# Logits of the second layer moved from TensorE to VectorE sums, with paired evictions, conditional weight splits and later ranks, in a pooled attention with two routed layers

## The chip, the cores and the metric

One core of one Trainium2 chip runs the whole program. The metric is the device time of one execution in microseconds; the median of three runs is given, and one profiled execution is read beside it. TensorE is PE in the profile, its weight load PEld, VectorE DVE, ScalarE ACT, GpSimd POOL and SyncE SP.

## The reference

An attention over keys and values that are pooled by eight gives x of 4608 tokens by 512. Two layers of eight experts follow, each expert 512 to 1024 to 512. Layer 1 gives a token to the expert of the largest logit; layer 2 passes a token by where its skip score is not positive, and adds to it otherwise.

```python
logits = x @ w_gate + modality_bias[modality_id]      # layer 1
e_idx = np.argmax(logits, axis=1)
...
h = np.maximum(x[mask] @ w1[e], 0.0)
out[mask] = gate_w[mask, None] * (h @ w2[e])
...
skip_score = x @ w_skip                               # layer 2, x = layer 1's output
do_compute = skip_score > 0
logits = xc @ w_gate
e_idx = np.argmax(logits, axis=1)
...
out[do_compute] = xc + y
```

Layer 2 so needs nine columns for every output row of layer 1: eight gate logits and the skip score.

## The kernel before, in words

The attention runs first; the routing of layer 1 begins beside it. A layer's tokens are sorted on chip into blocks of 256 rows (two halves, t = 0 and 1) that belong to one expert each, with the most used expert first. Layer 1 has 19 blocks with this input, from three experts. `Layer.second` does block 1, `Layer.body` the blocks from 2 on, `Layer.rec` those whose number is only known at run time; `first2` does layer 2's block 0 behind the last block of layer 1.

All products are made in fp32 as three products of high and low parts: each of w1, w2, x and h is split into a rounded high part (w1h, w2h, xh, hh, a copy on ACT) and the rest (w1l, w2l, xl, hl, a subtraction on DVE, for some w1l on POOL). `gemm1` (L1352) makes for each of eight slices f of the hidden width 12 matmuls of 128x256 into one of two PSUM buffers, from which ACT takes hh and DVE hl. `gemm2` (L1405) makes 24 matmuls of 128x512 for each half. In between, `xT` (L1311) transposes the next block's rows, and `split_w1`, `split_w2` (L1299, L1305) split the weights, in every block, even where the expert and so the raw weights stay the same: the loads of raw weights are conditional on a change of expert (chg), the splits are not. A half block skips its second `gemm2`.

The order of all instructions is written by hand: the program records them as the Python code runs, `body` calls `gemm1(i, f)`, then the split of w2, then a piece of the work that was deferred from the block before, for each f. The deferred work of layer 1's block i-1 (`deferred1`, L1561) is layer 2's gating for its outputs: `tr` transposes a half with PE (L1572), ACT and DVE split it (x2h, x2l); `mm` multiplies it with the gating weights W9s, high and low parts side by side in 64 columns (L1585); `mm2` transposes the result back (L1593) and DVE adds its two parts; `pick1` and `pick2` find on POOL and DVE the expert of each row (rt_mx and rt_my are the two maxima of DVE, M the one-hot choice, rt_i the running counts of POOL); x2 goes to DRAM and rows that skip are scattered to the output. `rank`, at the end of the block, multiplies M and rt_i with triangular and all-one matrices on PE (L874, L875, result R), DVE turns R into positions (L883 to L891), and POOL makes from them the one-hot tiles OB (L903).

```python
return {0: lambda: tr(0), 1: lambda: tr(1), 3: mm, 4: mm2, 5: pick1, 8: pick2, 9: rank}
```

The numbers are the f of gemm1 behind which each piece stands; 8 is the start and 9 the end of the second product. `body` gathers the rows of block i+1 at the start of block i (L1294), into one of two buffers xg. Layer 2 uses the same body with halves of a block chosen at run time, and no deferred work.

## Time and profile before

| | us |
|---|---|
| median of three runs | 990.66 (989.79 to 994.31) |
| the profiled execution's own time | 995.08 |
| its span in the trace | 993.3 |
| PE busy | 938.0 (94%) |
| DVE busy | 650.9 (66%) |
| ACT busy | 537.6 (54%) |
| POOL busy | 580.6 (58%) |

The profiled execution is one run of the program on the chip. Its mean granted clock of TensorE is 0.978 of full speed. The attention takes the first quarter, layer 1 runs to some 705 us, layer 2 to the end. A row of a timeline gives the start, the duration, the engine, the line, the operation, output and inputs with their tiles, the shape, how many alike follow in one row, and in brackets the idle time before it and what ended it. Matmuls are pipelined: their durations overlap, and the distance between two starts is what one costs.

### The profile page before, as it was taken

How to read it: one execution, taken by the hardware profiler on the slowest of the kernel's cores; microseconds unless marked ns; L12 is line 12 of the kernel's file. 1: busy time of each engine (PE TensorE's matmuls, PEld its weight loads, DVE VectorE, ACT ScalarE, POOL GpSimd, SP SyncE). 2: the span in 40 equal slices, each digit the busy share in tenths (PEclk: the TensorE clock that was granted, in tenths of full speed). 3: DMA queues.
4: the chain of work that ended last, by engine and by line, in shares of the span. 5: the costliest groups of instructions: out<-in, count | busy, mean ns of one | idle time of the engine just before them, and what ended most of it. 6: DMA issues, size and time to landing. Idle time of an engine off the chain costs nothing.

```text
span 993.3 us, 19808 instructions
## 1 busy us (share of the span) xinstructions
PE 938.0 (94%) x6535; PEld 841.5 (85%) x6535; DVE 650.9 (66%) x1533; ACT 537.6 (54%) x1137; POOL 580.6 (58%) x809
## 2 busy tenths in 40 slices
PE   5899999899999999999999999999898999999995
PEld 4699889788898888888899899988886897988984
DVE  4486786777666666666666676667546667667555
ACT  2465556544465555555566656546422555566553
POOL 4754697303587777677777777766634444342442
PEclk7799999999999999999999999999999999999998
DMA  9998865510111111442223521214422664481251
GB/s 225 216 253 228 230 181 161 182 55 23 44 60 66 57 63 58 137 144 72 71 74 101 186 75 61 70 60 155 153 76 79 222 219 163 132 282 34 96 173 40
DMA packets 86900, 123.66 MB, mean 124 GB/s; under 512 B 14143, under 2 KB 51007, under 8 KB 86760
## 3 DMA queue, kind: packets, MB, share of 16 engines
q1 hardware_dynamic: 75224, 94.31, 31.2%
q0 software_dynamic: 10320, 27.59, 8.9%
q8 instruction: 65, 1.06, 0.5%
q14 instruction: 75, 0.61, 0.2%
q10 hardware_dynamic: 1216, 0.08, 0.1%
HBM read 181.29 MB, written 39.48 MB: 222 GB/s over the span
## 4 chain that ended last, share of the span: by engine, by line
PE 69%; DMA 11%; DVE 7%; POOL 6%; issue 5%; ACT 2%; DVEq 0%; POOLq 0%; ACTq 0%
PE ps_g L1360 27%; PE ps_g L1412 23%; DMA out_dram<-o,o2i 5%; PE ps_av L368 4%; DMA xg<-xd,gidx 4%; PE ps_s L301 3%; PE ps_x L1314 2%; PE ps_lg L1585 2%; POOL OB L903 2%; PE ps_et L348 2%; PE ps_x L1572 1%; DMA xg<-x2s,gidx 1%; PE ps_s L327 1%; POOL w1l L1302 1%; PE ps_q L280 1%
## 5 line engine op out<-in xcount | busy, mean ns | idle before, releaser
L1360 PE MATMUL ps_g<-xh,w1h 128*128 128x256 f32 x896 | 262.0, 292 | 6.7 <-DVE hl L1364 3.8
L1360 PE MATMUL ps_g<-xl,w1h 128*128 128x256 f32 x896 | 253.4, 283 | 0.7 <-DVE xl L1318 0.7
L1360 PE MATMUL ps_g<-xh,w1l 128*128 128x256 f32 x896 | 253.6, 283 | 0.0
L1302 POOL TENSOR_TENSOR w1l<-w1r,w1h 128x512 fp32r<-128x512 f32 x105 | 134.3, 1303 | 103.8 <-ACT w1h L1301 103.0
L1412 PE MATMUL ps_g<-w2h,hh 128*128 128x512 f32 x464 | 189.7, 409 | 0.9 <-DVE rs_v L1038 0.5
L1363 ACT ACTIVATE hh<-ps_g 128x256 fp32r<-128x256 f32 x224 | 86.1, 384 | 188.9 <-PE ps_g L1360 183.3
L1412 PE MATMUL ps_g<-w2h,hl 128*128 128x512 f32 x464 | 183.4, 395 | 0.0
L1412 PE MATMUL ps_g<-w2l,hh 128*128 128x512 f32 x464 | 182.9, 394 | 0.0
L1360 PEld LDWEIGHTS ps_g<-xh,w1h 128*128 128x128 f32 x896 | 170.4, 190 | 14.5 <-issue 4.8
L1308 DVE TENSOR_TENSOR w2l<-w2r,w2h 128x512 fp32r<-128x512 f32 x232 | 160.4, 696 | 20.5 <-ACT w2h L1307 3.8
L1360 PEld LDWEIGHTS ps_g<-xl,w1h 128*128 128x128 f32 x896 | 170.8, 191 | 1.3 <-DVE xl L1318 1.1
L1360 PEld LDWEIGHTS ps_g<-xh,w1l 128*128 128x128 f32 x896 | 170.4, 190 | 0.0
L1364 DVE SCALAR_TENSOR_TENSOR hl<-ps_g,hh 128x256 fp32r<-128x256 f32 x224 | 94.9, 424 | 81.9 <-ACT hh L1363 79.9
L1307 ACT CAST w2h<-w2r 128x512 fp32r<-128x512 f32 x232 | 140.8, 613 | 2.6 <-DVE gidxf L1041 2.5
L1301 ACT CAST w1h<-w1r 128x512 fp32r<-128x512 f32 x240 | 136.8, 618 | 5.7 <-DMA w1r<-in_moe_w_dram 5.7
L903 POOL TENSOR_SCALAR OB<-iota,BB,pay 128x128 bf16<-128x128 bf16 x126 | 111.3, 891 | 20.9 <-DVE BB L891 18.5
L1302 DVE TENSOR_TENSOR w1l<-w1r,w1h 128x512 fp32r<-128x512 f32 x135 | 106.8, 814 | 9.3 <-ACT w1h L1301 9.1
L1412 PEld LDWEIGHTS ps_g<-w2h,hl 128*128 128x128 f32 x464 | 87.4, 188 | 21.6 <-DVE hl L1382 1.3
L1412 PEld LDWEIGHTS ps_g<-w2h,hh 128*128 128x128 f32 x464 | 87.6, 189 | 18.9 <-ACT hh L1381 1.5
L1412 PEld LDWEIGHTS ps_g<-w2l,hh 128*128 128x128 f32 x464 | 87.8, 189 | 16.1
L1318 DVE TENSOR_TENSOR xl<-ps_x,xh 128x512 fp32r<-128x512 f32 x64 | 43.9, 687 | 50.4 <-ACT xh L1317 50.3
L1557 POOL DMA_INDIRECT out_dram<-o,o2i x21 | 23.6, 1122 | 71.8 <-DVE o2i L1556 33.7
(280 smaller groups left out, 1487.0 us busy)
## 6 DMA issues: line engine op xcount, KB each, us to landing
w1r<-in_moe_w_dram SPq DMA_DIRECT2D x128, 512.0 KB
w2r<-in_moe_w_dram SPq DMA_DIRECT2D x128, 512.0 KB
x2s<-x SPq DMA_DIRECT2D x19, 522.0 KB
v<-in_v_dram SPq DMA_DIRECT2D x48, 192.0 KB
xd<-x SPq DMA_DIRECT2D x16, 520.0 KB
q_sb<-in_q_dram SPq DMA_DIRECT2D x16, 512.0 KB
kt<-in_k_dram SPq DMA_DIRECT2D x32, 144.0 KB
x2s<-OBx SPq DMA_DIRECT2D x16, 261.0 KB
```

What stands on the lines that cost most here:

```text
L301: nc.tensor.matmul(ps[p0:p1, hp // 2, (hp % 2) * 144:(hp % 2) * 144 + 144], lhsT=t[:, hp, p0:p1], rhs=KB[b % NR][:, hp, :], start=(hp % 2 ...
L368: nc.tensor.matmul(ps[p0:p1, j // 3, o:o + 2 * VW], lhsT=t[:, j, p0:p1], rhs=VB[b % NR][:, j].rearrange("p i w -> p (i w)"), start=(j % 3 ...
L903: e.tensor_scalar(g.ob(c)[:, i, :], g.iota, r.BB[:, c:c + 1], r.pay[:, i, c:c + 1], ALU.is_equal, ALU.mult)
L1301: self.nc.scalar.copy(self.w1h[f], raw)
L1302: (eng or self.nc.vector).tensor_tensor(self.w1l[f], raw, self.w1h[f].bitcast(F32), ALU.subtract)
L1307: self.nc.scalar.copy(self.w2h[f], raw)
L1308: (eng or self.nc.vector).tensor_tensor(self.w2l[f], raw, self.w2h[f].bitcast(F32), ALU.subtract)
L1318: nc.vector.tensor_tensor(self.xl[i % 2][:, :, 128 * t:128 * t + 128], ps, hi.bitcast(F32), ALU.subtract)
L1360: nc.tensor.matmul(ps, lhsT=a[f][:, k, :], rhs=b[:, k, :], start=(n == 0), stop=(n == 11))
L1363: nc.scalar.activation(out=self.hh[f], in_=ps, func=ACTF.Relu)
L1364: nc.vector.scalar_tensor_tensor(self.hl[f], in0=ps, scalar=0.0, in1=self.hh[f].bitcast(F32), op0=ALU.max, op1=ALU.subtract)
L1412: nc.tensor.matmul(ps, lhsT=a[f][:, tt], rhs=b[f], start=(n == 0), stop=(n == 23))
```

## The change

- Layer 2's nine columns are computed by DVE: for each half and column one `tensor_tensor_reduce` (`logit`) multiplies 128x512 rows of x2 with a broadcast row of the gating weights and sums them, 18 for a block. They stand in a list `todo` with their picks, from which `drip` takes some behind each f of gemm1 and gemm2. `settle` empties it for a block before its buffer x2 is written again. The gating weights are loaded during the attention, transposed once, and broadcast from DRAM to all partitions (`W9`, 9 by 512).
- hh and hl leave PSUM for two f at a time (128x512), and there are three PSUM buffers in place of two.
- In layer 1 the rows are gathered two blocks ahead; xh and xl have one buffer in place of two.
- In layer 1 w1 and w2 are split only if the next block has another expert (`split`), inside a branch on ACT and DVE; all w1l of layer 1 are now on DVE.
- `rank` of block i-1's outputs moves from the end of block i into block i+1, to gemm1's f = 4.
- In `first2` the second half's logits of the last block are made on PE (`late_logits`), the splits of w2 come three f later, two ranks stand in gemm1 (f = 4) and gemm2 (f = 2), and the transposes of block 1 inside gemm2(0, 0).
- In layer 2 the last split of w1 of a half block goes to POOL; the output tile o has two fixed buffers.

```diff
+        V.tensor_tensor(r.split, r.chg, r.end, ALU.add)
...
+        self.xh[1], self.xl[1] = self.xh[0], self.xl[0]
+        self.gate[1] = p.tile([128, 2], F32, name="gate1")
         for i in range(2):
             self.x2[i] = p.tile([128, 2, W2C], F32, name=f"x2{i}")
-        self.W9 = p.tile([128, 4, E + 1], F32, name="W9")
-        self.W9s = p.tile([128, 4, 64], F32R, name="W9s")
+            self.lg2[i] = p.tile([128, 2, E + 1], F32, name=f"lg2{i}")
+            self.dsi[i] = p.tile([128, 2], I32, name=f"dsi{i}")
+            self.rti[i] = p.tile([128, 2, E], BF16, name=f"rti{i}")
...
+        self.W9 = p.tile([128, E + 1, DM], F32, name="W9")
+        junk = self.sp.tile([128, DM], F32, tag="hr", name="junk", bufs=1)
+        self.junk = junk.bitcast(BF16)[:, 0:DM]
+        self.o2 = [p.tile([128, DM], F32, name=f"o2{t}") for t in range(2)]
...
+        nc, g = self.nc, self.g
+        ps = self.ps_t("ps_w")
+        for k in range(4):
+            nc.tensor.transpose(ps[0:E + 1, k, :], g.w9c[:, k, :], g.ident)
+        w = self.o2[0]
+        nc.scalar.copy(w[0:E + 1, :], ps[0:E + 1].rearrange("p k n -> p (k n)"))
+        nc.sync.dma_start(out=g.w9, in_=w[0:E + 1, :])
+        nc.sync.dma_start(out=self.W9, in_=g.w9.unsqueeze(0).to_broadcast([128, E + 1, DM]))
...
+    def load_split(self, i):
+        ET = mybir.EngineType
+        self.anew = self.nc.values_load(self.g.r1.split[0:1, i:i + 1], min_val=0, max_val=1,
+                                        engines=[ET.Activation, ET.DVE])
+    def split_w1_if(self, fs):
+        with self.tc.If(self.anew > 0):
+            for f in fs:
+                self.split_w1(f)
+    def split_w2_if(self, fs):
+        with self.tc.If(self.anew > 0):
+            for f in fs:
+                self.split_w2(f)
...
+            if f % 2 == 0:
+                self.ps_pair = self.ps_1("ps_g1")
+            out, whole = self.ps_pair[:, T * (f % 2):T * (f % 2) + T], self.ps_pair
+            hh, hl = (t[f // 4][:, f % 4 - 1:f % 4 + 1, :].rearrange("p f n -> p (f n)")
+                      if f % 2 else None for t in (self.hh4, self.hl4))
+        else:
+            out, whole, hh, hl = ps, ps, self.hh[f], self.hl[f]
...
+        if hh is not None:
+            nc.scalar.activation(out=hh, in_=whole, func=ACTF.Relu)
+            nc.vector.scalar_tensor_tensor(hl, in0=whole, scalar=0.0, in1=hh.bitcast(F32),
+                                           op0=ALU.max, op1=ALU.subtract)
-        return self.pp.tile([128, 512], F32, tag="g1", name=name, bufs=2)
+        return self.pp.tile([128, 512], F32, tag="g1", name=name, bufs=3)
...
+            self.settle(i - 2)
...
+            self.todo += self.posts(i, t)
...
+    def late_logits(self, i):
+        nc = self.nc
+        ps = self.ps_t("ps_x2")
+        for k in range(4):
+            nc.tensor.transpose(ps[:, k, :], self.x2[i % 2][:, 1, 128 * k:128 * k + 128],
+                                self.g.ident)
+        xt = self.o2[1].rearrange("p (k n) -> p k n", k=4)
+        nc.scalar.copy(xt, ps)
+        yield
+        lg = self.pp.tile([128, E + 1], F32, tag="m", name="ps_lg")
+        for k in range(4):
+            nc.tensor.matmul(lg, lhsT=xt[:, k, :], rhs=self.g.w9c[:, k, :], start=(k == 0),
+                             stop=(k == 3))
+        nc.vector.tensor_copy(self.lg2[i % 2][:, 1, :], lg)
...
+        self.gather(g.r2.gidx0, 2, 1, g.x2s[0:16 * T, :])
+        late = self.late_logits(n - 1)
         for f in range(8):
             self.gemm1(n, f)
+            for x in todo[2 * f:2 * f + 2 if f < 7 else None]:
+                x[2]()
+            if f in (1, 3):
+                next(late)
+            if f == 4:
+                self.rank_all(ranks)
+            if f == 5:
+                first()
+            if f > 2:
+                self.split_w2(f - 3)
+        second()
+        for f in range(5, 8):
             self.split_w2(f)
-            if f in d:
-                d.pop(f)()
-        self.gather(g.r2.gidx0, 2, 1, g.x2s[0:16 * T, :])
         self.gates1(1, self.sp)
-        d.pop(8)()
-        self.gemm2(0, 0, self.epilogue2)
-        for t in range(2):
-            self.xT(1, t, self.ps_t("ps_x"))
+        self.gemm2(0, 0, self.epilogue2, {2: self.rank_all,
+                                          3: lambda: self.xT(1, 0, self.ps_t("ps_x")),
+                                          5: lambda: self.xT(1, 1, self.ps_t("ps_x"))})
         self.gates2(1, self.sp)
         self.gemm2(0, 1, self.epilogue2)
-        d.pop(9)()
+        self.scatter(n - 1, 1)
...
+            P.tensor_copy(x2[:, :, DM:DM + E + 1], lg)
...
+            V.tensor_reduce(out=mx, in_=lg[:, :, 0:E], axis=AX.X, op=ALU.max)
+            P.tensor_tensor(eq, lg[:, :, 0:E], bc(mx), ALU.subtract)
+            P.tensor_scalar(eq, eq, 0.0, None, ALU.is_ge)
+            P.tensor_tensor(eq, eq, g.desc.unsqueeze(1).to_broadcast([128, 2, E]), ALU.mult)
...
+            V.tensor_reduce(out=my, in_=eq, axis=AX.X, op=ALU.max)
+            P.tensor_tensor(eq, eq, bc(my), ALU.subtract)
+            P.tensor_scalar(M, eq, 0.0, None, ALU.is_ge)
...
+            self.ranks.append(i)
...
+    def rank(self, i):
+        nc, g, r2 = self.nc, self.g, self.g.r2
+        V = nc.vector
+        M, I = r2.M[:, 2 * i:2 * i + 2, :], self.rti[i % 2]
+        B = r2.BB[:, 2 * i:2 * i + 2]
+        R = self.pp.tile([128, 2, E], F32, tag="m", name="R")
...
+        nc.gpsimd.tensor_tensor(r2.RH[:, 2 * i:2 * i + 2], ra, B, ALU.subtract)
+        for _ in route_places(self.tc, g, r2, 2 * i, 2, nc.gpsimd):
+            pass
...
+    def logit(self, i, t, e):
+        self.nc.vector.tensor_tensor_reduce(
+            out=self.junk, in0=self.x2[i % 2][:, t, 0:DM], in1=self.W9[:, e, :], scale=1.0,
+            scalar=0.0, op0=ALU.mult, op1=ALU.add, accum_out=self.lg2[i % 2][:, t, e:e + 1])
+    def posts(self, i, t):
+        l = [(i, True, partial(self.logit, i, t, e)) for e in range(E + 1)]
+        if t == 0 and i > 0:
+            l.insert(5, (i - 1, False, partial(self.scatter, i - 1, 1)))
+        if t == 1:
+            first, second = self.picks(i)
+            l += [(i, True, first), (i, True, second)]
+        return l
+    def settle(self, i):
+        while any(x[0] <= i for x in self.todo):
+            self.drip()
+    def drip(self, n=1):
+        while n > 0 and self.todo:
+            _, cost, f = self.todo.pop(0)
+            f()
+            n -= cost
...
+        ahead = 2 if self.n == 1 else 1
+        if i + ahead < NBLK:
+            self.gather(i + ahead)
...
+    def body1(self, i, end):
+        m = self.m
+        late = i == self.n_static - 1
+        ranks = m.ranks
+        m.ranks = []
+        for f in range(8):
+            m.gemm1(i, f)
+            if f in (1, 3):
+                m.split_w2_if(range(2 * f - 2, 2 * f + 2))
+            m.drip(((0, 0, 1, 1, 1, 1, 2, 2) if late else (1, 1, 1, 2, 1, 2, 1, 1))[f])
+            m.g.bg.tick()
+            if f == 4:
+                m.rank_all(ranks)
+        if late:
             m.gather2(i + 1)
             m.load_w1_parts(2, m.e2, end, range(4))
-        self.finish(i, d, end, full, turn)
+        full = self.load_full(i)
+        more = i + 1 < NBLK or end is not None
+        if i + 1 < NBLK:
+            self.load_w2(i + 1)
+        if end is not None:
+            m.load_w2_parts(2, m.e2, end)
+        def next_x(t):
+            if t == 0 and end is not None:
+                m.gates1(i + 1, m.sp)
+            m.xT(i + 1, t, m.ps_t("ps_x"))
+            if t == 1:
+                m.gates2(i + 1, m.sp)
+        if more:
+            m.load_split(i + 1)
+            if end is None:
+                m.gates1(i + 1, m.sp)
+            m.split_w1_if(range(8))
+        at = {f: m.drip for f in (0, 1, 3, 5, 6)}
+        if more and not late:
+            at.update({2: lambda: next_x(0), 4: lambda: next_x(1)})
+        m.gemm2(i, 0, self.epilogue, at)
+        if more and late:
+            m.drip(4)
+            next_x(0)
+            next_x(1)
+            m.drip(3)
+        else:
+            m.drip(7)
+        with m.tc.If(full > 0):
+            m.gemm2(i, 1, self.epilogue)
```

PE in a block of layer 1. Before, the rank (R, from M and rt_i) opens the first product, whose matmuls (ps_g) are broken by two groups of four transposes and by the logits:

```order
L874 MATMUL R<-M_666,trim 128x16
L875 MATMUL R<-rt_i,ones 128x16
L1360 MATMUL ps_g_3639<-xh_2114,w1h_2120 128x256
...
L1572 MATMUL ps_x_3656<-ident,x_2998 128x128 x4
L1360 MATMUL ps_g_3665<-xh_2114,w1h_2120 128x256
...
L1572 MATMUL ps_x_3682<-ident,x_2998 128x128 x4
...
L1585 MATMUL ps_lg<-x2h,W9s 64x256
...
L1585 MATMUL ps_lg<-x2l,W9s 64x256
L1360 MATMUL ps_g_3734<-xh_2114,w1h_2532 128x256
...
L1593 MATMUL ps_lt<-ident,lt 128x64 x2
L1360 MATMUL ps_g_3756<-xh_2114,w1h_2532 128x256
```

Now nothing but the rank of an earlier block stands between the matmuls, behind f = 4:

```order
L1400 MATMUL ps_g_4008<-xh_2117,w1l_2538 128x256
L1696 MATMUL R<-M_669,trim 128x16
L1697 MATMUL R<-rti_3003,ones 128x16
L1400 MATMUL ps_g_4008<-xh_2117,w1h_2537 128x256
```

The transposes and logits are gone, and R moved from the block's start into its first product.

DVE in the same block, around the first product's start. Before, each hl (128x256) is followed by a w2l:

```order
L1364 SCALAR_TENSOR_TENSOR hl_2535<-ps_g_4844,hh_2534 128x256
L1308 TENSOR_TENSOR w2l_2991<-w2r_2539,w2h_2990 128x512
L1364 SCALAR_TENSOR_TENSOR hl_2535<-ps_g_4861,hh_2534 128x256
L1308 TENSOR_TENSOR w2l_2993<-w2r_2539,w2h_2992 128x512
L1336 TENSOR_REDUCE g_mx<-xg_2113 128x2
L1337 TENSOR_TENSOR gd_3004<-xg_2113,g_mx 128x2x8
L842 TENSOR_REDUCE rt_my<-rt_eq 128x2
L1318 TENSOR_TENSOR xl_2115<-ps_x,xh_2114 128x4x128
L1302 TENSOR_TENSOR w1l_2121<-w1r_2118,w1h_2120 128x512
```

Now hl is 128x512, the splits stand behind a branch, and the logits (ISA, each with the read of its 128x1 sum) fill the queue:

```order
L1717 ISA lg_3001 128x1
L1405 SCALAR_TENSOR_TENSOR hl_2126<-ps_g_6008,hh_2125 128x512
L1335 COMPARE_AND_BRANCH
...
L1335 UNCONDITIONAL_BRANCH x2
L1717 ISA junk,lg_3001<-x_3000,W_3008 128x512
L1717 ISA lg_3001 128x1
...
L1325 TENSOR_LOAD split_650
L1370 TENSOR_REDUCE g_mx<-xg_2116 128x2
L1330 COMPARE_AND_BRANCH
L1320 TENSOR_TENSOR w1l_2124<-w1r_2120,w1h_2123 128x512 x2
...
L1330 UNCONDITIONAL_BRANCH x2
L1717 ISA junk,lg_3001<-x_3000,W_3008 128x512
...
L1352 TENSOR_TENSOR xl_2118<-ps_x,xh_2117 128x4x128
```

The subtractions of w1l and w2l moved into the branch; in front of xl there are logits in place of hl and w2l.

PE in `first2`, in the second product of layer 2's block 0. Before, the next block's transposes stand between the halves and the rank behind both:

```order
L1412 MATMUL ps_g_14767<-w2h_2992,hl_2535 128x512
L1314 MATMUL ps_x<-ident,xg_2721 128x128 x8
L1412 MATMUL ps_g_14816<-w2h_2540,hh_2122 128x512
...
L1412 MATMUL ps_g_14816<-w2h_2992,hl_2535 128x512
L874 MATMUL R<-M_666,trim 128x16
L875 MATMUL R<-rt_i,ones 128x16
```

Now the rank comes behind the third slice of the first half, ahead of the transposes:

```order
L1453 MATMUL ps_g_14603<-w2h_2720,hl_2126 128x512
L1696 MATMUL R<-M_669,trim 128x16
L1697 MATMUL R<-rti_3007,ones 128x16
L1453 MATMUL ps_g_14603<-w2h_2722,hh_2125 128x512
...
L1453 MATMUL ps_g_14603<-w2h_2722,hl_2126 128x512
L1348 MATMUL ps_x<-ident,xg_2726 128x128 x4
L1453 MATMUL ps_g_14603<-w2h_2724,hh_2539 128x512
```

The rank moved ahead by some 40 matmuls, and the transposes into the first half.

## Rows read from the trace of the kernel before

**Rows 1.** Busy time per engine in two stretches of one block.

```profile
core 0: us, PE busy (x) PEld busy (x) DVE busy (x) ACT busy (x) POOL busy (x), PEclk, DMA share, GB/s
438.40:464.30 25.90, 25.90 (x174) 23.33 (x173) 16.70 (x38) 15.28 (x32) 18.98 (x30) 1.00 0.24 83
541.80:567.60 25.80, 25.80 (x173) 23.27 (x172) 16.58 (x38) 15.29 (x32) 18.92 (x30) 1.00 0.59 192
```

**Rows 2.** Timeline of PE in one block of layer 1.

```profile
start us, us, engine line op out<-in xcount [idle before <-releaser]
446.23 0.60 PE L1572 MATMUL ps_x<-ident,x 128*128 128x128 f32 x4
...
446.90 0.28 PE L1360 MATMUL ps_g<-xh,w1l 128*128 128x256 f32 x1
...
451.37 0.28 PE L1585 MATMUL ps_lg<-x2h,W9s 128*64 128x256 f32 x1
...
452.31 0.28 PE L1360 MATMUL ps_g<-xh,w1h 128*128 128x256 f32 x1
...
453.63 0.28 PE L1360 MATMUL ps_g<-xh,w1l 128*128 128x256 f32 x1
...
454.44 0.28 PE L1360 MATMUL ps_g<-xh,w1l 128*128 128x256 f32 x1
```

**Rows 3.** Timeline of DVE in the same block; columns as in Rows 2.

```profile
445.12 0.17 DVE L885 TENSOR_REDUCE rt_ra<-rt_rk 128x2 f32<-128x16 f32 x1
445.33 0.17 DVE L887 CAST rt_ri<-rt_ra 128x2 int32<-128x2 f32 x1
...
447.41 0.69 DVE L1308 TENSOR_TENSOR w2l<-w2r,w2h 128x512 fp32r<-128x512 f32 x1
448.02 0.69 DVE L1578 TENSOR_TENSOR x2l<-ps_x,x2h 128x512 fp32r<-128x512 f32 x1
...
463.09 1.52 DVE L1302 TENSOR_TENSOR w1l<-w1r,w1h 128x512 fp32r<-128x512 f32 x1
```

**Rows 4.** Timeline of DVE in layer 2; columns as in Rows 2.

```profile
772.12 0.74 DVE L1553 SCALAR_TENSOR_TENSOR o<-ps_g,gate,xg 128x512 f32<-128x512 f32 x1
772.78 0.14 DVE L1556 TENSOR_TENSOR o2i<-xg,emptyf 128x1 int32<-128x1 f32 x1
772.85 0.16 DVE L1349 TENSOR_REDUCE g_su<-gd 128x2 f32<-128x18 f32 x1
```

**Rows 5.** Timeline of POOL, layer 1 and first2; columns as in Rows 2.

```profile
446.75 3.82 POOL L903 TENSOR_SCALAR OB<-iota,BB,pay 128x128 bf16<-128x128 bf16 x4
...
456.01 0.26 POOL L1606 TENSOR_SCALAR d_pos<-x 128x2 f32<-128x2 f32 x1 [2.60 <-DVE x L1597]
...
457.85 0.22 POOL L832 TENSOR_TENSOR rt_eq<-x,rt_mx 128x16 f32<-128x16 f32 x1
...
458.51 0.52 POOL L836 TENSOR_TENSOR rt_eq<-rt_eq,desc 128x16 f32<-128x16 f32 x1
...
731.26 0.21 POOL L844 TENSOR_TENSOR rt_eq<-rt_eq,rt_my 128x16 f32<-128x16 f32 x1 [3.07 <-DVE rt_my L842]
...
733.00 0.19 POOL L870 CAST rt_i<-carry 128x8 bf16<-128x8 f32 x1
```

**Rows 6.** DVE groups by shape: xcount | busy us, mean ns | idle.

```profile
L1159 DVE SCALAR_TENSOR_TENSOR tokf<-rs_v,rs_lo 128x52 f32<-128x52 f32 x2 | 0.4, 213 | 0.1
...
L999 DVE SCALAR_TENSOR_TENSOR er_a<-RH,er_a 128x18 f32<-128x18 f32 x1 | 0.2, 178 | 0.0
```

**Rows 7.** Waits of PE by what they were for: us, times, longest.

```profile
PE ps_g L1360 <- DVE hl L1364: 3.8, 5, 1.1
```

**Rows 8.** PE timeline, block 13 to 14; columns as in Rows 2.

```profile
568.77 0.17 PE L874 MATMUL R<-M,trim 128*128 128x16 bf16 x1 [0.28 <-POOL M L848]
570.55 0.17 PE L875 MATMUL R<-rt_i,ones 128*128 128x16 bf16 x1 [1.61 <-POOL rt_i L870]
```

**Rows 9.** Stretch of PE after that; columns as in Rows 1.

```profile
572.00:575.00 3.00, 3.00 (x16) 3.00 (x16) 2.93 (x4) 1.44 (x3) 2.80 (x4) 0.50 0.23 87
```

**Rows 10.** PE timeline, step into first2; columns as in Rows 2.

```profile
708.22 0.55 PE L1360 MATMUL ps_g<-xh,w1h 128*128 128x256 f32 x1 [2.58 <-issue]
```

More of the change, by code (lines that the diff above doesn't have):

```diff
@@ L1117, in route_blocks @@
     yield
+    if r.split is not None:
+        V.tensor_tensor(r.split, r.chg, r.end, ALU.add)
+        yield
 def route_slots(tc, g, r, sp, pp, pace=1):
@@ L1521, in gather_next @@
         self.gather(gi, 0, i, g.x2s[0:16 * T, :])
+    def late_logits(self, i):
[6 more added lines that the diff above has]
+        nc.scalar.copy(xt, ps)
+        yield
+        lg = self.pp.tile([128, E + 1], F32, tag="m", name="ps_lg")
[3 more added lines that the diff above has]
+        nc.vector.tensor_copy(self.lg2[i % 2][:, 1, :], lg)
+        yield
     def first2(self, n):
         nc, g = self.nc, self.g
+        ranks = self.ranks
+        self.ranks = []
+        todo = [x for x in self.todo[:-11]]
+        first, second = self.picks(n - 1)
+        self.todo = []
         nc.vector.tensor_copy(self.gate0, self.gate[n % 2])
@@ L1619, in pick2, with second @@
+        def second():
+            eq, val = st["eq"], st["val"]
+            my = tile("rt_my")
+            V.tensor_reduce(out=my, in_=eq, axis=AX.X, op=ALU.max)
+            P.tensor_tensor(eq, eq, bc(my), ALU.subtract)
+            P.tensor_scalar(M, eq, 0.0, None, ALU.is_ge)
+            P.tensor_tensor(M, M, bc(val), ALU.mult)
+            for c in range(2):
+                P.tensor_tensor(r2.carry, r2.carry, M[:, c, :], ALU.add)
+                P.tensor_copy(I[:, c, :], r2.carry)
             nc.sync.dma_start(
@@ new lines, in rank_all @@
+    def rank_all(self, ranks=None):
+        ranks = self.ranks if ranks is None else ranks
+        while ranks:
+            self.rank(ranks.pop(0))
+    def logit(self, i, t, e):
[10 more added lines that the diff above has]
+        return l
@@ L1684, in second @@
         self.gather(2)
+        if self.n == 1:
+            self.gather(3)
         if self.n == 2:
@@ L1723, in body @@
             m.load_w1_parts(2, m.e2, end, range(4))
-        d = self.deferred(i - 1, nc.gpsimd) if self.deferred is not None else {}
-        def gemm1():
-            for f in range(8):
-                m.gemm1(i, f)
-                m.split_w2(f)
-                if f in d:
-                    d.pop(f)()
-                m.g.bg.tick()
         full = turn = None
         if self.n == 1:
-            gemm1()
+            self.body1(i, end)
         else:
@@ L1829, in finish @@
-        deferred_at(8)
-        late = i == self.n_static - 1
-        m.gemm2(i, 0, self.epilogue,
-                {2: lambda: next_x(0), 4: lambda: next_x(1)} if more and not late else {})
-        if more and late:
-            next_x(0)
-            next_x(1)
-        if more:
-            last_splits()
-        with tc.If(full > 0):
-            m.gemm2(i, 1, self.epilogue)
-        deferred_at(9)
+        at = {}
+        with tc.If(full > 0) as cmp:
+            if more:
+                at = {2: lambda: next_x(0), 4: lambda: next_x(1)}
+            m.gemm2(i, 0, self.epilogue, at)
+            if more:
+                m.split_w1(4)
+                m.split_w1(5)
+                m.gates_exp()
+                m.split_w1(6, pool)
+                m.split_w1(7, pool)
+                m.gates2(i + 1, m.sp)
+            m.gemm2(i, 1, self.epilogue)
@@ new lines, in finish, with early, turn_x @@
+        with cmp.Else():
+            def early():
+                m.split_w1(2)
+                m.split_w1(3)
+            def turn_x(t):
+                m.xT(i + 1, t, m.ps_t("ps_x"))
+                m.split_w1(4 + t)
+                if t == 1:
+                    m.gates1(i + 1, m.sp, False)
+            if more:
+                at = {3: early, 4: lambda: turn_x(0), 6: lambda: turn_x(1)}
+            m.gemm2(i, 0, self.epilogue, {1: turn, **at})
+            if more:
+                m.gates_exp()
+                m.split_w1(6)
+                m.split_w1(7, pool)
+                m.gates2(i + 1, m.sp)
```

240 lines of the change are left out of this document (79 added, 161 removed).

## The prediction

> **What bounds the kernel now.** I read the busy time by stretch first, then the timelines of each engine through one block of layer 1, then the waits of PE. In a stretch of one block PE is busy for all of it, 25.90 of 25.90 us, while DVE works 16.70, ACT 15.28 and POOL 18.98, at a granted clock of 1.00 [rows 1]. A stretch in which a new expert's weights arrive, with a DMA share of 0.59 instead of 0.24, takes no longer [rows 1]. So layer 1 is bound by PE's instruction stream, and an instruction taken from PE shortens the block as long as no other engine comes to need more than what is left. That is the question here: the change takes work from PE and puts a longer piece on DVE.
>
> **What leaves PE.** The logits of layer 2 cost PE three pieces in each block [rows 2]. The row of four transposes begins at 446.23, and the third matmul behind it at 446.90 instead of two steps of 0.12 later: 0.43 us, twice in a block. The eight logit matmuls run from 451.37 to 452.31: 0.94. Around the two small transposes, three matmuls take from 453.63 to 454.44 instead of 0.36: 0.45. Together 2.25 us, so a block bound by PE falls from 25.85 to 23.6. With 19 blocks that is 42.8. The last half block keeps its logits on PE: 0.43 for four transposes, and for four matmuls at most half of 0.94; 0.9 goes back. **Term: -41.9 us.**
>
> **What comes to DVE.** Each block gets 18 logit sums of 128x512, each followed by a 128x1 read of the accumulator. The trace has no such pair, so the step L from one sum to the next must be bounded. A 128x512 operation on the same operands (w2l) is busy 0.69 us and the next starts 0.61 us after it [rows 3]. A 128x1 operation is busy 0.14 us behind a 128x512 one, and the next starts 0.07 us after it [rows 4]. A handover between dependent small operations costs 0.04 (busy 0.17, next start after 0.21) [rows 3]. Lower end: 0.61 + 0.07 = 0.68, if nothing waits. Upper end: 0.69 + 0.14 + 2 x 0.04 = 0.91, if both handovers are waited out. The next sum waits for the read, while the read needs no data of the sum through memory, so I take 0.61 + 0.14 + 0.04 = 0.79; both ends stay in the range.
>
> DVE's block is then: 18 x 0.79 = 14.2; four paired hl and two xl at 0.61 [rows 3], 3.7; eleven small operations (gates, maxima, rank) at 0.20, 2.2; one register load and three branches, of which no row in layer 1 tells, between 0.2 and 1.3, taken as 0.6. Between the two maxima of a pick (mx and my) DVE must wait for POOL: two copies (some 0.5), five operations from 456.01 to 457.85, and three to 459.03 [rows 5], 3.5 us in all, of which 0.2 is mx itself. The sum is 24.0 us against PE's 23.6. The two engines are level, with DVE slightly behind: 0.3 in each of the 14 blocks without a change of expert. **Term: +4 us.** What leaves DVE in these blocks (eight w2l, about five w1l, two x2l) is already out of that sum.
>
> **The blocks that do change expert.** The transfers show two in layer 1 (into blocks 9 and 14). There 16 subtractions come back, 16 x 0.61 = 9.8 us [rows 3], and now all of them on DVE, eight of them ahead of the xl on which PE's next first product waits. In a level schedule there is no slack for them. The bounds are 0 and 9.8; three logits (2.4) stand behind xl and can slip, so I take 7. Block 13, ahead of the second change, is a half block: PE skips 24 matmuls of about 0.23, 5.6 us, but DVE computes all 18 logits. There the deficit is 9.8 + 5.6, and I take 15. **Term: +22 us.** Before, these splits were made in every block under PE's cover and cost nothing.
>
> **Stalls that go.** [...] Waits of the first product for hl, 3.8 us in five waits [rows 7], are in layer 2, where the third PSUM buffer removes most: **-3**. The new long waits at the two changes bring the low clock back behind them, at 1.5 each [rows 9]: **+3**. POOL loses its w1l in layer 1; nothing waited for those, so nothing is gained by that alone. The earlier gathers, the broadcast of the gating rows (2.4 MB, once, before block 1) and ACT's lighter load I cost at nothing: ACT is at 15.28 of 25.90, and DMA at 0.24 [rows 1]; without that cover the broadcast would hold the first logits, not PE.
>
> **The step into layer 2.** The last rank stands inside gemm2(0,0) at f=2, 2.1 us after the first product's end. On POOL the previous rank's four OB (3.82) come first, then the picks (3.5), then the chain from rt_my to the last rt_i, 731.26 to 733.19 [rows 5]. Starting from the rank at f=4 (7 us into the product, plus 1.2 on DVE), M and I are ready at 7 + 1.2 + 3.8 + 3.5 + 1.9 = 17.4, while PE comes to R at 11.4 + 2.1 = 13.5: a wait of 3.9, bounded by 0 and 5. Before, R stood at the end and did not wait. [...] The 2.58 us on the way into this code [rows 10] stay; for the new branches on that way I add 1. **Term: +6.**
>
> **Sum.** -41.9 + 4 + 22 - 3.4 - 3 + 3 + 6 = -13.3 us. The profiled execution took 995.08, 4.4 above the median of the runs shown; from its time the change gives 981.8, from the median 990.66 it gives 977. I forecast 977, 1.3% faster. A measurement of this kernel can tell about 0.5%, so 985.7 to 995.6 counts as no change.
>
> [...] Operations of two f32 tensors in SBUF with a second arithmetic step show, between 18 and 52 elements, 178 and 213 ns [rows 6]: 1.03 ns an element, and none of them writes an accumulator. [...]
>
> **Rivals.**
> 1. *Half rate of the sums (slower).* If an accumulating sum takes twice as long for an element, a step grows by 512 x 1.03 ns = 0.53 to 1.32. DVE's block is 33.5 us, 7.7 above today's 25.85, or about 130 us over 17 blocks: some 1,110 to 1,120. For it: no row has the accumulator. Against it: the rows of 1.03 ns. Chance 0.07.
> 2. *DVE becomes the bound (same to slower).* Each 0.01 us of L beyond 0.79 costs 18 x 17 x 0.01 = 3.1 us, since DVE is already level with PE. From L = 0.83 on the gain is below 0.5%; at 0.85 it is gone, above it the kernel is slower, and 0.88 gives 1,005. For it: two handovers by semaphore in every pair. Against: the pipelined step of 0.61. Chance 0.24.
> 3. *POOL and DVE in each other's way (slower).* A w1l on DVE took 1.52 instead of 0.69 while POOL did a w1l [rows 3]. If the four OB of a block held up a logit each by 0.83, that is 3.3 a block, 56 over 17, some 1,030. Against it: two w2l inside OB's 446.75 to 450.57 were not longer (447.41: 0.69) [rows 3, 5]. Chance 0.04. [...]
> 4. *The stalls are smaller (faster still).* With L at 0.70 DVE has 1.3 us of slack a block, the pace term vanishes, and the changes cost 10 instead of 22: 950 to 962. Chance 0.12.
> 5. *The splits are not skipped.* If the flag were set in every block, DVE would carry 9.8 us more in each: 33.8, as slow as the first rival. The routing writes the flag from the change of expert and the two changes are seen in the transfers, so 0.03.
>
> **How the numbers follow.** My forecast, L from 0.70 to 0.83, has 0.50 and gives 962 to 985. Of the second rival's 0.24, 0.02 is still faster by 0.5%, 0.14 lies within it and 0.08 is slower. Faster: 0.50 + 0.12 + 0.02 = 0.64; the same: 0.14; slower: 0.08 + 0.07 + 0.04 + 0.03 = 0.22. The range goes from 957 (the better part of the fourth rival) to 1,003 (most of the second); beyond its ends lie the first, third and fifth rivals and the rest of the fourth.
>
> **What would show it.** In the changed profile: no transposes and no 64-column logits on PE in blocks 2 to 17; a period of 23.6 to 24.2; the start of one logit sum to the next 0.79; PE waits for xl into blocks 9 and 14 of 2 to 10 us, with a clock of 0.50 behind them; a wait at R in gemm2(0,0). Wrong would be a logit step over 0.85 with PE waiting for hl in every block, or no wait at the changes.

## The result, and the profile after

The changed kernel takes 976.84 us (median of four runs, 975.85 to 977.64); the kernel before, run four times, 991.69 (989.79 to 994.31). The ratio is 0.9855, with a 95% interval of 0.9835 to 0.9875: 1.45% faster. The forecast was 977. The profiled executions went from 995.08 to 976.46, their spans from 993.3 to 974.7.

The page's busy times and granted clock of the changed kernel:

```profile
PE 906.6 (93%) x6209; PEld 811.9 (83%) x6209; DVE 694.3 (71%) x1842; ACT 372.9 (38%) x733; POOL 510.7 (52%) x763
...
PEclk7799999999999999999999899998999999999997
```

PE works 31.4 us less and is idle 12.8 us more: 974.7 - 906.6 = 68.1, before 993.3 - 938.0 = 55.3. ACT falls from 537.6 to 372.9, and DVE rises from 650.9 to 694.3. A steady block of layer 1, the stretch at the start of block 14, and a part of that stretch, by engine:

```profile
core 0: us, PE busy (x) PEld busy (x) DVE busy (x) ACT busy (x) POOL busy (x), PEclk, DMA share, GB/s
492.31:515.95 23.64, 23.64 (x157) 21.33 (x157) 18.03 (x54) 5.16 (x9) 13.84 (x27) 1.00 0.23 81
553.00:561.00 8.00, 3.92 (x18) 3.73 (x19) 5.77 (x18) 0.54 (x1) 5.53 (x18) 0.57 0.26 100
557.46:560.70 3.24, 3.24 (x15) 3.24 (x16) 3.07 (x11) 0.00 (x0) 2.72 (x5) 0.50 0.00 0
```

The block takes 23.64 us instead of 25.85 and PE is busy throughout, as before [rows 1]: the 23.6 that was forecast. DVE's records cover 18.0 of it. The second row is what the change of expert costs: in 8 us PE works 3.92. The granted clock is 0.57 there, since it is 0.50, as in [rows 9], from 553.9 to 560.7. Up to 557.46 PE waits and loses nothing by that; in the 3.24 us of the third row it works at 0.50, where two matmuls of 128x256 start 0.21 us apart, 0.12 from 560.77 on. By the clock half of that time is lost, 1.6 us (by the distances 1.4); below, time at 0.50 is counted by the clock, an estimate.

The sums in DVE's timeline, each with the read of its accumulator:

```profile
436.11 0.69 DVE L1717 CUSTOM_DVE_ANT_0 junk<-x,W 128x512 bf16<-128x512 f32 x1
436.73 0.08 DVE L1717 DVE_READ_ACCUMULATOR2_ANT lg<- 128x1 f32 x1
436.85 0.69 DVE L1717 CUSTOM_DVE_ANT_0 junk<-x,W 128x512 bf16<-128x512 f32 x1
...
452.12 0.82 DVE L1717 CUSTOM_DVE_ANT_0 junk<-x,W 128x512 bf16<-128x512 f32 x1
```

From 436.11 to 436.85 is 0.74 us a step, where 0.79 was taken between 0.68 and 0.91 [rows 3, 4]: the sum is 0.69 busy, as w2l is, the read 0.08. The read starts 0.07 before its sum's end (436.73), and the next sum 0.04 behind the read's end (436.85). All 333 of each average 703 and 81 ns in the view by shape. Beside POOL's OB a sum is 0.82 long (452.12).

PE's waits in the changed kernel, those in layer 1 and at the start of layer 2:

```profile
PE ps_x L1348 <- DMA xg<-x2s,gi: 4.9, 1, 4.9
PE ps_g L1400 <- DVE xl L1352: 4.8, 3, 4.1
...
PE R L1696 <- POOL M L1671: 4.2, 1, 4.2
PE ps_g L1453 <- DVE hl L1405: 3.5, 2, 2.6
...
PE R L1697 <- POOL rti L1674: 2.5, 2, 1.6
PE R L1696 <- DVE rt_rk L1701: 2.4, 1, 2.4
PE ps_g L1400 <- ACT xh L1351: 2.4, 1, 2.4
```

The waits of the first product for hl [rows 7] and the waits of block 14 for R [rows 8] are gone; the 24.7 us of this list are mostly new. PE from block 13 to 14, and DVE in that place:

```profile
553.00 0.38 PE L1400 MATMUL ps_g<-xh,w1h 128*128 128x256 f32 x1 [2.38 <-ACT xh L1351]
557.46 0.58 PE L1400 MATMUL ps_g<-xl,w1h 128*128 128x256 f32 x1 [4.08 <-DVE xl L1352]
```

```profile
548.37 4.91 DVE L1320 TENSOR_TENSOR w1l<-w1r,w1h 128x512 fp32r<-128x512 f32 x8 [0.83 <-ACT w1h L1319]
...
553.89 0.69 DVE L1352 TENSOR_TENSOR xl<-ps_x,xh 128x512 fp32r<-128x512 f32 x1
556.64 0.17 DVE L1668 TENSOR_REDUCE rt_my<-rt_eq 128x2 f32<-128x16 f32 x1 [2.06 <-POOL rt_eq L1662]
556.72 0.68 DVE L1352 TENSOR_TENSOR xl<-ps_x,xh 128x512 fp32r<-128x512 f32 x1
```

In block 14 PE waits 2.38 us for xh and 4.08 for xl. On DVE eight w1l (4.91 us) stand ahead of the first xl, and between the two xl stands rt_my, which waits 2.06 us for POOL.

### The profile page after: what moved, and what is told of

Its sections match the earlier page's. It is cut to its first block, busy times and chain, and to the rows that moved or that the text cites. A ratio compares the mean times of both kernels' runs of the same rounds, so it can differ in the third digit from the quotient of the medians.

```text
span 974.7 us, 19004 instructions
## 1 busy us (share of the span) xinstructions
PE 906.6 (93%) x6209; PEld 811.9 (83%) x6209; DVE 694.3 (71%) x1842; ACT 372.9 (38%) x733; POOL 510.7 (52%) x763
## 5 line engine op out<-in xcount | busy, mean ns | idle before, releaser
L1400 PE MATMUL ps_g<-xh,w1h 128*128 128x256 f32 x896 | 255.1, 285 | 2.4 <-ACT xh L1351 2.4
L1717 DVE CUSTOM_DVE_ANT_0 junk<-x,W 128x512 bf16<-128x512 f32 x333 | 234.2, 703 | 19.1 <-DVEq L1335 5.4
L1404 ACT ACTIVATE hh<-ps_g 128x512 fp32r<-128x512 f32 (+1 forms) x116 | 67.7, 583 | 251.3 <-PE ps_g L1400 239.6
L1405 DVE SCALAR_TENSOR_TENSOR hl<-ps_g,hh 128x512 fp32r<-128x512 f32 (+1 forms) x116 | 77.6, 669 | 58.8 <-ACT hh L1404 39.3
L1320 POOL TENSOR_TENSOR w1l<-w1r,w1h 128x512 fp32r<-128x512 f32 x40 | 51.7, 1312 | 60.8 <-ACT w1h L1319 60.5
L1342 DVE TENSOR_TENSOR w2l<-w2r,w2h 128x512 fp32r<-128x512 f32 x112 | 75.4, 709 | 7.2 <-ACT w2h L1341 6.0
L1683 POOL DMA_INDIRECT out_dram<-x,dsi x38 | 46.8, 1232 | 50.7 <-DMA out_dram<-x,dsi 18.0
L1319 ACT CAST w1h<-w1r 128x512 fp32r<-128x512 f32 x120 | 68.1, 619 | 5.9 <-DMA w1r<-in_moe_w_dram 5.4
L1513 ACT ACTIVATE x<-ps_g,gate 128x512 f32<-128x512 f32 x37 | 25.5, 690 | 106.7 <-PE ps_g L1453 99.5
L1341 ACT CAST w2h<-w2r 128x512 fp32r<-128x512 f32 x112 | 63.8, 617 | 3.3 <-DVE gidxf L1044 2.5
```

What stands on the lines that cost most here:

```text
L1319: self.nc.scalar.copy(self.w1h[f], raw)
L1320: (eng or self.nc.vector).tensor_tensor(self.w1l[f], raw, self.w1h[f].bitcast(F32), ALU.subtract)
L1341: self.nc.scalar.copy(self.w2h[f], raw)
L1342: (eng or self.nc.vector).tensor_tensor(self.w2l[f], raw, self.w2h[f].bitcast(F32), ALU.subtract)
L1400: nc.tensor.matmul(out, lhsT=a[f][:, k, :], rhs=b[:, k, :], start=(n == 0), stop=(n == 11))
L1404: nc.scalar.activation(out=hh, in_=whole, func=ACTF.Relu)
```

## The experiments

All times of a group are from one chip and share runs of the kernel before; ratios to it are compared, since the kernel before itself ran at 991.5 to 994.3 in these groups.

### Splits in every block

```diff
-        with self.tc.If(self.anew > 0):
-            for f in fs:
-                self.split_w1(f)
+        for f in fs:
+            self.split_w1(f)
```

(and split_w2 alike)

> The splits of w1 and w2 in layer 1 are made in every block again, without the branch; all else as in the changed kernel. My theory: skipping them is what makes room for the sums on VectorE. In a steady block VectorE waits some 2.5 us for TensorE; 16 subtractions of 0.61 us are 9.8 us more, so about 7 us a block over 14 to 15 blocks: 1,080 us (1,055 to 1,110), with TensorE waiting for hl or xl in every block. Rival: TensorE's products still cover the splits, as they did before the change: 977 to 985 us.

Measured: 1104.02 us, ratio 1.1117 (1.1085 to 1.115). PE's waits, and the stretch of one block of layer 1 (columns as above):

```profile
PE ps_g L1398 <- DVE xl L1350: 48.6, 17, 6.1
PE ps_g L1451 <- DVE hl L1403: 20.2, 20, 2.9
```

```profile
626.47:657.17 30.70, 21.25 (x133) 19.04 (x132) 27.23 (x70) 12.44 (x25) 15.55 (x28) 0.83 0.35 122
```

A block takes 30.7 us, 7.1 more than 23.6, and PE waits in each for xl, 48.6 us in all, and for hl. DVE is busy for 27.2 of the 30.7 us, and the granted clock falls to 0.83. With the splits in every block the rest of the change makes the kernel 11% slower: what pays for the sums is that most blocks skip the splits. The rival falls.

### Four sums more in each block

```diff
-        l = [(i, True, partial(self.logit, i, t, e)) for e in range(E + 1)]
+        l = [(i, e >= 2, partial(self.logit, i, t, e % (E + 1))) for e in range(E + 1 + 2)]
```

> Four sums more in each block of layer 1 (two columns of each half are computed twice), 4 x 0.735 = 2.9 us of VectorE. Theory after the result: VectorE has some 2.5 us of slack in a steady block (its waits for hl), so a block grows by 0 to 0.5 us, and the stalls at the two changes of expert by some 3 each: 985 us (978 to 995). Rival, the prediction's own term: VectorE is level with TensorE, and each microsecond on it is a microsecond of the block: 17 x 2.9 = 50, some 1,025 us.

Measured: 1011.5 us, ratio 1.0186 (1.0153 to 1.0219), between the theory's range and the rival's time. The first rows are the R of two blocks in the middle of layer 1, the others PE's waits:

```profile
511.85 0.17 PE L1697 MATMUL R<-rti,ones 128*128 128x16 bf16 x1
...
535.73 0.17 PE L1697 MATMUL R<-rti,ones 128*128 128x16 bf16 x1
```

```profile
PE ps_g L1453 <- DVE hl L1405: 11.2, 8, 5.0
PE ps_g L1400 <- DVE xl L1352: 8.5, 6, 3.9
PE R L1696 <- DVE rt_rk L1701: 7.7, 1, 7.7
```

The blocks there take 23.9 us, 0.25 more for 2.94 us of work: DVE's slack in a steady block is some 2.7 us, not -0.3 as the prediction had it. The loss is in other places: the second rank waits 7.7 instead of 2.4, the blocks ahead of it take 1.2 to 2.0 us more, and the waits at the two changes of expert grow. So the slack theory holds for the steady block and missed that DVE's delay is paid wherever PE waits for one particular step in DVE's queue.

### The weights split in halves, and the pick behind xl

```diff
-            m.split_w1_if(range(8))
+            m.split_w1_if(range(4))
...
                 m.gates2(i + 1, m.sp)
+                m.split_w1_if(range(4, 8))
```

> The branch that splits w1 for a new expert is made two branches: four slices before the second product, four behind the transposes of its f = 4. Theory: the waits of TensorE at the start of block 14 (2.38 for xh, 4.08 for xl) come from the eight splits that stand ahead of xh and xl on ScalarE and VectorE; with four of them later the waits fall to 1 to 3 us and the low clock behind them shrinks: 968 to 973 us. Rival: the pick's wait for GpSimd between the two xl sets the time: 976 to 978.

Measured: 975.61 us, ratio 0.9817 (0.9793 to 0.9841); the changed kernel has 0.9855 and, repeated, 0.9868. The start of block 14, and gemm2 after it:

```profile
555.19 0.58 PE L1400 MATMUL ps_g<-xl,w1h 128*128 128x256 f32 x1 [3.72 <-DVE xl L1352]
...
574.66 0.50 PE L1453 MATMUL ps_g<-w2h,hl 128*128 128x512 f32 x1 [1.32 <-DVE hl L1405]
...
577.64 0.50 PE L1453 MATMUL ps_g<-w2h,hl 128*128 128x512 f32 x1 [0.87 <-DVE hl L1405]
```

The wait for xh is gone (2.38 to 0.15), that for xl is 3.72 instead of 4.08, and the w1l that were put off come back as waits of the second product for hl, 1.32 and 0.87. By the ratios the halves give 4 to 5 us, but the intervals all but touch, and the time lies in neither range. At block 14 the waits fall by 1.3 (6.46 + 0.89 before, 3.87 + 2.19 now), and even that is not gained: from the R of block 13 to that of block 15 it is 51.54 us (539.84 to 591.38), in the changed kernel 51.63 (539.53 to 591.16).

What differs more is a place that the theory did not name, the step into layer 2. PE's wait for layer 2's first gather (gi), 4.93 us in the changed kernel, is 0.38 here, although no gather was moved. The rows are PE here, then the scatter ahead of the gathers in POOL's queue, in the changed kernel and here:

```profile
673.95 0.33 PE L1348 MATMUL ps_x<-ident,xg 128*128 128x128 f32 x1 [0.38 <-DMA xg<-x2s,gi]
```

```profile
665.75 0.98 POOL L1683 DMA_INDIRECT out_dram<-x,dsi  x1 [6.23 <-DVE lg L1717]
661.76 1.24 POOL L1683 DMA_INDIRECT out_dram<-x,dsi  x1 [2.54 <-DVE lg L1717]
```

The scatter waits 2.54 us for a sum of DVE instead of 6.23, so the gathers behind it start some 4 us earlier. Why it is released earlier was not isolated. R's waits behind it grow, from 4.16 to 2.20 + 6.10, and the profiled execution as a whole gains nothing (span 975.4, the changed kernel 974.7).

```diff
-        at = {f: m.drip for f in (0, 1, 3, 5, 6)}
+        at = {f: m.drip for f in (0, 1, 5, 6, 7)}
```

> In the second product of layer 1's blocks, deferred pieces stand behind f = 0, 1, 5, 6, 7 in place of 0, 1, 3, 5, 6, so that the second maximum of a pick, which waits for GpSimd, comes behind both xl. Theory: of the 4.08 us that TensorE waits for xl into block 14, 2.06 are VectorE's wait for GpSimd between the two xl, and they go; elsewhere in the list nothing is late: 2 to 4 us below the changed kernel, 0.981 to 0.985 of the kernel before. Rival: the splits ahead of xl set the wait alone: 0.986 to 0.988.

Measured: 974.46 us, ratio 0.9821 (0.9804 to 0.9839), in the theory's range. PE at the start of block 14, in an execution that took 981.64, 7 above the median:

```profile
553.98 0.38 PE L1400 MATMUL ps_g<-xh,w1h 128*128 128x256 f32 x1 [2.24 <-ACT xh L1351]
...
556.20 0.58 PE L1400 MATMUL ps_g<-xl,w1h 128*128 128x256 f32 x1 [1.84 <-DVE xl L1352]
```

The wait for xl falls from 4.08 to 1.84, by 2.24 against the 2.06 of DVE's wait for POOL. The time falls by less: from the R of block 13 to that of block 14 it is 25.42 us (540.65 to 566.07) instead of 26.47 (539.53 to 566.00), as PE now works at a granted clock of 0.50 from 556.2 to 562.4 and loses 3.1 us by it instead of 1.6.

### Two PSUM buffers

```diff
-        return self.pp.tile([128, 512], F32, tag="g1", name=name, bufs=3)
+        return self.pp.tile([128, 512], F32, tag="g1", name=name, bufs=2)
```

> Two PSUM buffers for the first product's pairs in place of three. Theory: with pairs, two buffers leave VectorE one pair's time (2.9 us) to take hl out, and sums and splits stand ahead of it in its queue, so waits for hl come back, some 0.5 us in many blocks of layer 1 and more at the changes: 980 to 990 us. Rival: the third buffer gives nothing, and the waits for hl went because of the pairs: 976 to 978.

Measured: 979.79 us, ratio 0.9868 (0.9839 to 0.9897): no different from the changed kernel, so neither theory is refuted by the time. The waits tell more:

```profile
PE ps_g L1400 <- DVE hl L1405: 3.6, 1, 3.6
```

It is one wait of 3.6 us, in the block behind the first change of expert, not small waits in many blocks, as the theory had it. In layer 2, where four of the five waits for hl stood before [rows 7], there is none with two buffers either, so it is not the third buffer that removed them; the pairs are the likely reason, but no run tests them alone. At the change of expert the third buffer gains nothing here: from the R of block 8 to that of block 10 it is 53.43 us with two buffers (414.57 to 468.00) and 53.67 with three (414.96 to 468.63), where the waits for the counts and for hl (1.59 and 2.62) take the place of the 3.6.

### Three steps moved, one at a time

The changed kernel was run again as the yardstick.

> The changed kernel itself, unaltered, as the yardstick of this group on the same chip: 976 to 979 us.

Measured: 981.45 us, ratio 0.9868 (0.9845 to 0.9892), 2.5 us above the range expected. Its profiled execution has R's wait in first2 at 8.87 us instead of 4.16:

```profile
697.15 1.06 POOL L1312 DMA_INDIRECT xg<-x2s,gidxf  x1 [3.17 <-DMA out_dram<-x,dsi]
...
703.96 3.13 POOL L906 TENSOR_SCALAR OB<-iota,BB,pay 128x128 bf16<-128x128 bf16 x4
...
711.29 0.49 POOL L1671 TENSOR_TENSOR M<-M,d_val 128x16 bf16<-128x16 bf16 x1
```

```profile
711.83 0.17 PE L1696 MATMUL R<-M,trim 128*128 128x16 bf16 x1 [8.87 <-POOL M L1671]
```

On POOL four gathers stand from 697.15 to 703.7, then OB (3.13), then the picks that make M at 711.29, for which PE waits at 711.83.

```diff
-            if f == 4:
-                m.rank_all(ranks)
+            if f in (4, 6) and ranks:
+                m.rank(ranks.pop(0))
+        m.rank_all(ranks)
```

> Where two ranks fall into one block, the second stands at f = 6 of the first product in place of f = 4. Theory: the second R waits 2.43 us for the VectorE step that reads the first R, because R has one PSUM buffer and three sums stand ahead of that step; apart they wait for nothing: 2 to 4 us less than the changed kernel (the low clock behind it included). Rival: the two ranks' work on GpSimd and VectorE is the same and the wait comes back elsewhere: within 1 us of it.

Measured: 975.7 us, ratio 0.982 (0.9796 to 0.9844), 5.8 below the yardstick, more than expected. The wait of 2.43 us for rt_rk is gone from the list, and with it the low clock behind it (1.7 us in the yardstick, from 365 to 370; in the first profile of the changed kernel the granted clock is 1.00 there, from 350 to 380). The rest is R's wait in first2, 5.65 in this execution instead of 8.87; it differs from run to run, and nothing shows that the move changed it.

```diff
-        self.gemm2(0, 0, self.epilogue2, {2: self.rank_all,
-                                          3: lambda: self.xT(1, 0, self.ps_t("ps_x")),
+        self.gemm2(0, 0, self.epilogue2, {3: lambda: self.xT(1, 0, self.ps_t("ps_x")),
...
-        self.gemm2(0, 1, self.epilogue2)
+        self.gemm2(0, 1, self.epilogue2, {1: self.rank_all})
```

> In first2 the last rank stands at f = 1 of the second half's product, gemm2(0, 1), in place of f = 2 of the first half's. Theory: TensorE's wait for M and the counts (4.16 + 0.90 us) goes with the low clock behind it (1.7): 4 to 7 us less than the changed kernel. Rival: the rank is what the routing of layer 2 waits for; moved by 7 us it delays the gather for layer 2's block 2 by as much, and TensorE's wait there (2.56) grows: within 1.5 us of it or slower.

Measured: 973.24 us, ratio 0.9802 (0.9775 to 0.9828), 8.2 below the yardstick, more than expected, as R's wait was 8.87 in the yardstick and not 4.16. No R waits in first2; one of 1.96 us takes its place:

```profile
707.79 0.50 PE L1453 MATMUL ps_g<-w2l,hh 128*128 128x512 f32 x1 [1.96 <-DVE w2l L1342]
...
742.93 1.09 PE L1348 MATMUL ps_x<-ident,xg 128*128 128x128 f32 x4 [3.67 <-issue]
```

The second row is the gap ahead of the transposes of layer 2's block 2, 3.67 us; in the yardstick it is 3.73. So nothing downstream was late: against this place the rank's early place gained nothing.

```diff
+        after = self.n == 1 and i >= self.n_static
+        if after:
+            m.gather_next(i + 1)
         if i + ahead < NBLK:
             self.gather(i + ahead)
```

(and the later gather_next left out)

> In the blocks whose number is known at run time, the gather for layer 2's block 0 is issued ahead of layer 1's gather for two blocks on, in place of behind it. Theory: TensorE's wait of 4.93 us at the transposes of layer 2's block 0, which was 0.62 before the change, comes from the GpSimd queue: the gathers stand 3.2 us behind two others that are for a block that does not exist: 2.5 to 6 us less than the changed kernel. Rival: the gather lands when the write of x2s and the weight loads let it, 6.7 us behind its issue: within 1 us of it.

Measured: 978.73 us, ratio 0.9829 (0.9794 to 0.9864), 2.7 below the yardstick, the lower end of what was expected, with intervals that overlap. The wait of 4.5 us for xg by gi is gone from the trace, but two others are new or longer, behind a new one of 1.00 for xl:

```profile
696.88 0.18 PE L1696 MATMUL R<-M,trim 128*128 128x16 bf16 x1 [2.12 <-DVE lg L1581]
...
713.38 0.17 PE L1696 MATMUL R<-M,trim 128*128 128x16 bf16 x1 [9.80 <-POOL M L1671]
```

R in first2 waits 9.80 here, 0.93 more than in the yardstick. Of the 4.5 us, 4.0 come back in these three waits: what is gained ahead of a step that waits for another engine is given back at it, as long as that step stays where it is. The order of the gathers is also not the only thing that removes the wait for gi: with w1 split in halves it was 0.38 without this move.

### The moves together

> The moves of the three kernels before (second rank at f = 6, last rank in gemm2(0, 1), next gather first) with w1 split in halves. Theory: each removes a wait of its own, so they add up: 5 to 6 for the last rank, 2.4 for the second rank, 4.5 for the gather and 1 to 3 for the halves, with their low clocks some 14 to 19 us below the changed kernel: 0.967 to 0.973 of the kernel before. Rival: one wait takes the other's place, since GpSimd's queue is behind most of them: 0.976 to 0.980.

Measured: 963.0 us, ratio 0.9714 (0.9701 to 0.9727), where the changed kernel has 0.9855; it is 2.9% faster than the kernel before: the fastest of all runs, inside the theory's range. Against the changed kernel that is 14 us by the ratios, less than the 21 that the single results add up to (5.8, 8.2, 2.7 and 4), since the difference in R's wait in first2 counts in the first two. PE's waits in layer 1 and behind it:

```profile
PE ps_g L1453 <- DVE hl L1405: 4.8, 4, 2.5
...
PE ps_g L1400 <- DVE xl L1352: 4.4, 3, 3.7
...
PE R L1696 <- POOL rti L1673: 2.4, 1, 2.4
PE R L1695 <- DVE lg L1581: 1.9, 1, 1.9
```

The waits for gi, for M and for rt_rk are gone; for gi the halves or the moved gather can be the cause. What is left in layer 1 are mostly the changes of expert (xl 3.73, the counts 2.43, hl 4.8 in all).

> All of these moves together, the pick's second maximum behind both xl as well. Theory: 2 to 4 us less than the kernel with the three moves and halves, 0.964 to 0.971 of the kernel before. Rival: no less than that one.

Measured: 967.49 us, ratio 0.9767 (0.9749 to 0.9785): 4.5 slower, so the rival holds. The wait for xl does fall (3.73 to 1.51), but in first2 the transposes of block 1 wait 3.49 us for their gather, which they did not in the other, and the product around them 3.27 for w2l instead of 1.57. Whether the later pick is what delays these was not isolated; the profiled execution took 964.27, and so shows only 1.3 of the 4.5.

### The tail

```diff
-                m.split_w1(7, pool)
+                m.split_w1(7)
```

> The changed kernel with the last split of w1 of layer 2's half blocks on VectorE again, as before the change. From TensorE's last matmul to the end of the span the changed kernel takes 13.8 us, the one before 10.9. Theory: the 1.27 us split stands behind the last scatter in GpSimd's queue and holds the end: 1 to 3 us less in this tail. Rival: the tail is longer for another reason (the way out of the program): 13 us and more.

Measured: 974.0 us, ratio 0.9815 (0.98 to 0.983). The last rows of PE and POOL in the changed kernel, then in this one:

```profile
960.53 0.40 PE L1453 MATMUL ps_g<-w2h,hl 128*128 128x512 f32 x1
```

```profile
964.88 1.27 POOL L1320 TENSOR_TENSOR w1l<-w1r,w1h 128x512 fp32r<-128x512 f32 x1
```

```profile
968.48 0.40 PE L1453 MATMUL ps_g<-w2h,hl 128*128 128x512 f32 x1
```

```profile
971.41 1.39 POOL L1632 DMA_INDIRECT out_dram<-o,o2i  x1 [5.12 <-POOLq L1918]
```

From the end of the last matmul (960.93 of a span of 974.7; 968.88 of 980.0) it is 13.8 and 11.1 us, 2.7 less, as the theory has it. But the split, which is for a block that does not exist, accounts for its own 1.3 only: of the other kernels, all with the split on POOL, most have a tail of 13.1 to 14.0, but the next gather first has 11.9 (966.50 to 978.4) and the moves together 11.6 (949.56 to 961.2) and 11.9 (950.57 to 962.5). What sets the rest of the tail stays open.

## Why the prediction was right, point by point

- **What leaves PE, -41.9.** Right: a steady block went from 25.85 to 23.64.
- **What comes to DVE, +4.** Wrong in size: nothing was paid in the steady blocks. (The prediction's own sum gives 0.4 us a block, not 0.3, and with its price of 3.1 us for each 0.01 of the step, 0.83 gives 989 and not the 985 at which its forecast ends.) The step is 0.74, not 0.79, which is 0.9 us a block, and DVE has 2.7 us to spare there (the experiment with four sums more). Most of the rest is the wait between the two maxima: 3.3 was taken, about 2 are seen (2.06 at 556.64). The 0.6 for the register load and the branches, for which the prediction had no row, is near what shows: 10.1 us idle behind branches ahead of sums (5.4 + 4.7), 0.6 in each of 17 blocks. The half rate of the first rival is not seen: 703 ns for 512 elements with two f32 sources in SBUF and an accumulator, against 696 for w2l.
- **The blocks that change expert, +22.** At block 14 the place and the mechanism were right, the size too large; at block 9 PE does not wait for xl, as predicted, but for the counts and for hl. In block 9 the waits are 1.59 (R) and 2.62 (hl), at block 14 they are 2.38, 4.08 and 0.89, 11.6 in all; DVE's slack of 2.7 a block is a likely reason for the difference. The clock behind them costs the 3 taken: PE works at a granted clock of 0.50 from 451.5 to 454.9 and from 557.46 to 560.7, 3.3 us lost. Together 14.9 for 25. At block 14 the order of the pick, which the term did not have, is 2 of the waits.
- **Stalls that go, -3.4 and -3.** Right: the -3.4, 0.28 and 1.61 us of waits for R at block 14 [rows 8] and 1.5 for the 3 us at a granted clock of 0.50 after them [rows 9], is gone with R's wait there, and so are 3.8 us of waits for hl, but not by the third PSUM buffer that the prediction named: with two they stay away too.
- **The step into layer 2, +6.** Right for the profiled execution (4.16 + 0.90, and 1.7 by the clock, 0.50 from 710.9 to 714.4, for which the +6 counts 1.5, half of the 3 us of [rows 9]), from the queue that was named (OB, picks, chain). But the four gathers, which stand ahead of OB in that queue, were left out, and so it varies: 8.87 in the repeated run, 9.80 with the gather moved. The 1 us for new branches was wrong in sign: PE's 2.58 us on the way into first2 [rows 10] does not appear any more, nor the low clock behind it.
- **What was not in the sum.** Two ranks in one block, 2.43; the gather for layer 2's block 0, behind two others in POOL's queue, 4.93 instead of 0.62, and 2.7 by the clock behind it (PE works at a granted clock of 0.50 from 678.25 to 683.6); the tail, 2.9 (13.8 against 10.9), of which 1.3 is the split behind the last scatter. The prediction priced the earlier gathers at nothing, because DMA had room (a share of 0.24 [rows 1]); what they cost is their place in POOL's queue, where the scatter's wait of 6.23 us for DVE also stands ahead of them.

Terms in the trace come to -41.9 + 14.9 - 3.6 - 3.8 + 6.8 - 4.3 + 2.4 + 7.0 + 2.9 = -19.6, of a difference in span of -18.6. Waits outside of this list moved as well (at the transposes of layer 2's later blocks PE waited 6.0 us, now 2.6; behind a wait of 0.77 at 643.92 the granted clock is newly 0.50, from 646.1 to 649.5), so the terms are no better than 1 to 2 us. The forecast's -13.3 came near since three errors to the dear side (DVE's pace, the changes, the way into first2), 19 us together, outweighed three terms that it did not have, 12 us. That the total agrees is luck in so far; the bound by PE, the sums' pace within its bounds, the stalls at block 14 and the wait at R in first2 are not. The rival of a longer step falls with 0.74, the half rate with 703 ns, the splits that are not skipped with the first experiment, which shows what that would have been.

## What to carry to other kernels

When work moves from the bounding engine to one that also makes operands in time for it, compare the receiver's load per block, but also walk its queue in the blocks that differ from the steady one: there the stalls were here, 11.6 us at the two changes of expert. Moving a step to an earlier place is only a gain if something waits for it; here a rank that was moved ahead by some 40 matmuls cost 5 to 11 us (its waits in the runs above) and saved nothing against the later place that was tried. And an operation whose result nothing needs still takes its place in the queue: here two gathers for a block that does not exist stood for 3.2 us (667.06 to 670.28) ahead of the one for layer 2's block 0, for which PE waited 4.93 us instead of 0.62. A wait that goes in a trace is not yet time gained: at block 14 the halves took 1.3 us of waits away, and the two blocks took as long as before.
